# One fused attention and feed-forward kernel: two blocks of the last chunk written directly, a new written order, more adding on VectorE

## The chip, the cores and the metric

The kernel runs on one core of one Trainium2 chip. The metric is device time in microseconds (us) for one execution, the median of several runs. Beside it there is one execution recorded by the hardware profiler; its span runs from the core's first to its last instruction and is a little shorter than its time. Engines: PE (TensorE, matmuls), DVE (VectorE), ACT (ScalarE), POOL (GpSimd), SP (SyncE, which here only issues transfers).

## The reference

x has S = 2048 rows of D = 640 values in bf16. Three weight matrices make queries, keys and values for 32 heads of 20 values each; every row attends to W = 8 rows, itself and the 2nd, 4th, ... 14th row before it. Beside the attention runs a feed-forward layer of F = 1536 hidden values.

```python
x = A_x
xn = _layernorm(x)                                   # no scale, no bias
qkv = xn @ wqkv                                      # (2048, 3*640), 32 heads of 20
idx = pos[:, None] - 2 * arange(8)[None, :]          # masked where negative
logits = einsum("bhsd,bhswd->bhsw", q, kg) * 20**-0.5
o = einsum("bhsw,bhswd->bhsd", softmax(logits), vg)
ffn = gelu(xn @ w1 + b1) @ w2 + b2
return x + o @ wo + ffn
```

## The kernel before

The 2048 rows are cut into four chunks (n = 0 to 3) of 512 rows, each of four blocks of 128 rows. All weights and all of x stay on the chip. The work of a chunk is a chain of pieces, each a Python function of a few instructions with a short name; in the names the first digit is the chunk.

- st, su, sq, rs, rc, xn: layer norm of a block (statistics on DVE for chunks 0 and 1, on ACT for 2 and 3). tp and tc turn a normed block so that features lie on partitions (chunk 0: on PE, with copies; the others: a transposing transfer that SP issues, L292).
- hj and hc (chunk 0), pj and pc (the others): the projections to queries (first digit after the chunk or after hj: 0), keys (1) and values (2) on PE, and ACT's copies of them out of PSUM. ga to ge and gc are the first two blocks' queries.
- qk: DVE multiplies queries with shifted keys (L433) into two large buffers, half[0] and half[1], one for each four of the eight offsets. Five values of a head are on different 128-column tiles and must still be added: PE sums over partitions with a matmul against head_of (L479, piece lg), and either sums over the tiles as well by accumulating, or DVE adds tiles first. LEVEL[n] says how far DVE goes: at 0 PE takes five tiles, at 1 DVE adds two pairs (pa, L465) and PE takes three, at 2 one more add (pb, L470) and PE takes two, at 3 yet one more and PE takes one.
- m, mx, ex, ss, ri, at: the softmax over eight offsets (maximum, subtraction, exponential, sum, reciprocal, product). Chunk 0 does it in two parts, a and b. The exponentials and the logarithms use one table of ACT, the GELU another; changing between them is a load (L173).
- xd, xs: SP's transfers that copy each head's weights to the four partitions of the head (L563). av: DVE multiplies them with shifted values (L578). ad, ot: four DVE adds of the halves (L587, L592), whose result oT is the attention output, features on partitions.
- f1, ge: the hidden layer on PE (L599) and its GELU on ACT (L615); twelve tiles a chunk.

The outputs of chunks 0 to 2 are made turned: piece t(n)(s)(0 to 3) accumulates the hidden layer's part of 128 output columns s, t(n)(s)4 the attention's part, which needs oT (L673). u copies the result out of PSUM with b2 (ACT, L676), ut turns it back by a transposing transfer that SP issues (L680), and ud adds it onto the output in memory by an accumulating transfer that POOL issues (L685). The output rows have been filled with x before (xp).

The last chunk's outputs are made straight, block by block (bl = 0 to 3), so that nothing has to be turned at the end: o3(bl)(0 to 3) is the hidden layer's part, o3(bl)4 the attention's. A row of 640 columns takes two PSUM places, lo with 512 columns and hi with 128. For blocks 0, 1 and 2, oc copies both out on ACT (L641, L642) and od adds them to the output through POOL (L646). The last block is written directly: xl has added b2 to its x rows, oclo adds x to lo on DVE (L693) and stores 512 columns through SP (L694); ohi makes the last 128 columns on PE, ochi adds x to them (L702) and ochd stores them through ACT's queue (L707).

PSUM has eight places: psA gives four by turns to all that is tagged acc, psO two, psL one tile of two places to the logits.

The order is written out by hand: ORDER (L41 to L71) lists all pieces, and PE, DVE, ACT and SP each take the instructions of the pieces in that order, every one waiting for its inputs. A piece may hold instructions of more than one engine; oclo holds an add of DVE and a transfer of SP. In chunk 1, for instance, u13 stands in L63, u12 in L64, ut12 in L65 and ut13 in L66. POOL is not in the set of engines that keep the written order (L810); the tool that builds the program orders its instructions itself.

Of the kernel before, what the change touches and what calls it, by code (L numbers as in the profile page):

```python
# [46 lines left out]
pj113 pc113 pj103 pj111 ge0_10 pj101 pc111 pj114 ldx ge0_7 pa000 pc101 pa010 lg0 mask m0a ld2 pc103 pj102 pc114 pad11
su21 mx0a ex0a pj112 pc112 m0b mx0b ss0a pc102 ex0b ri0a ss0b pj100 pc100 at0a ri0b at0b pj110 pj104 pc104 pc110 xd0
qk111 f10_2 ge0_2 su22 qk100 hj212 hc212 f10_6 ge0_6 pj121 su20 f10_1 pc121 su23 ldo f11_10 ge1_10 ng2 ge0_1 sq20
f11_5 f10_11 pj122 pc122 f10_3 qk110 sq22 t040 qk101 f11_0 t000 lg1 xp0 av010 ge0_3 sq21 xs0 ge1_0 sq23 rs2 f10_8  # L50
ge0_8 t001 m1 f11_3 rc2 xn23 tc23 ge0_11 av031 t041 mx1 av021 xn20 tc20 f11_7 av011 ge1_5 ge1_7 av001 ge1_3 xp1 f10_9
t042 t002 xn21 ge0_9 tc21 pj120 xn22 tc22 av030 av000 f11_9 ge1_9 pj124 ex1 av020 ss1 pc120 pc124 pj123 pc123 ad00 ri1
t043 f11_2 t003 pj204 at1 pc204 xd1 su31 ad01 pad12 ad02 ot0 pj200 pc200 pj201 pc201 av101 xp2 pj212 su30 pc212 pj220
pj213 pc220 pc213 pj223 pc223 pj211 su33 pc211 pj203 su32 ng3 sq33 pad21 av100 sq31 pj202 f11_6 t004 u00 av110 xs1
av130 t044 av120 av131 av121 t010 av111 t011 t012 t013 u04 t020 t014 sq32 pc203 pc202 pj221 sq30 rs3 rc3 ad11 u01 ut00
ad10 ad12 t030 pj210 pc221 t031 t021 t022 ut01 ge1_2 pj214 xn33 tc33 t032 t033 t034 xn31 tc31 ge1_6 pj224 t023 t024
f11_8 ot1 pc214 pad22 pc210 qk201 qk211 qk210 xn30 tc30 f12_9 qk200 f11_1 pa210 pa201 xn32 ge1_8 u02 pa211 pa200 f11_4
ge1_1 t100 ge1_4 tc32 pj311 pc311 pb212 ud00 ud01 ge2_9 pj310 pc310 pad31 pj304 pc304 pj314 pc314 t101 pj300 pj324
pc324 ut02 pj303 f12_10 pb202 pc224 u03 pc303 xp3 pj301 pc301 xl ge2_10 pc300 f13_9 pj313 pc313 pj312 ud02 ut03 ud03
pj302 pc302 f13_6 ge3_6 pj323 lg2 pc312 qk300 m2 pc323 f11_11 ge1_11 f13_0 ge3_0 mx2 ut04 f13_11 ge3_9 ex2 pa300 ss2  # L60
qk310 ri2 at2 xs2 qk301 t130 t131 f12_1 ge2_1 ge3_11 t132 f13_10 qk311 t102 t103 f13_2 pa310 xd2 t104 pj320 pc320
f13_1 ge3_1 u10 ut10 ud10 f12_8 pa311 pa301 pb312 ge2_8 f13_8 ge3_8 t110 t133 t111 t112 t113 t114 u11 ge3_10 f12_5
pj222 pc222 pj321 pc321 pb302 lg3 av200 t134 u13 m3 av221 ge2_5 xb3 f12_11 t140 t141 t120 ut11 mx3 f12_2 ge3_2 av211  # L63
ex3 ss3 ri3 av220 ge2_2 f13_5 ge2_11 t142 t143 t121 t122 t123 f12_6 ge2_6 at3 xs3 f12_3 ge2_3 t124 u12 f12_7 pj322  # L64
ud04 av210 av201 av231 f12_0 t144 ge2_7 ge2_0 t200 av230 pc322 u14 ut12 ud11 f12_4 ge2_4 ge3_5 f13_4 ge3_4 o310 f13_7  # L65
ge3_7 t210 ad20 ad21 ad22 ot2 f13_3 t201 t202 pad32 av321 t203 ge3_3 o311 av331 ut13 av320 xd3 t204 u20 av300 ut14  # L66
# [8 lines left out]
def kernel(  # L75
# [544 lines left out]
    def do_o(n, bl, pc, parts):  # L620
        cs = slice(bl * P, (bl + 1) * P)
        if pc == 0 and "lo" in parts:
            for part in ("lo", "hi"):
                pool, tag = (psA, "acc") if bl % 2 else (psO, "o")
                tiles[part, n, bl] = pool.tile([P, CH], F32, tag=tag, name=part)
        lo, hi = tiles["lo", n, bl], tiles["hi", n, bl]
# [4 lines left out]
        for k, (lhs, rhs) in enumerate(srcs):
            first, last = pc == 0 and k == 0, pc == 4 and k == len(srcs) - 1
            if "lo" in parts:
                nc.tensor.matmul(lo[:], lhsT=lhs, rhs=rhs[:, 0:CH], start=first, stop=last)  # L634
            if "hi" in parts:
                nc.tensor.matmul(hi[:, 0 : D - CH], lhsT=lhs, rhs=rhs[:, CH:D], start=first, stop=last)  # L636

    def do_oc(n, bl):
        osb = outp.tile([P, D], BF16, tag="osb", name="osb")
        tiles["osb", n, bl] = osb  # L640
        nc.scalar.copy(osb[:, 0:CH], tiles["lo", n, bl][:])  # L641
        nc.scalar.copy(osb[:, CH:D], tiles["hi", n, bl][:, 0 : D - CH])  # L642

    def do_od(n, bl):
        b = n * BPC + bl
        nc.gpsimd.dma_start(out_sd[b * P : (b + 1) * P, :], tiles["osb", n, bl][:], accum_op=ALU.add)  # L646
# [41 lines left out]
    last = (NCH - 1, BPC - 1)  # L688

    def do_oclo():  # L690
        osb = outp.tile([P, D], BF16, tag="osb", name="osb")
        tiles["osb", last] = osb
        nc.vector.tensor_tensor(out=osb[:, 0:CH], in0=tiles["lo", *last][:], in1=x_sb[:, LASTB, 0:CH], op=ALU.add)  # L693
        nc.sync.dma_start(out_sd[LASTB * P :, 0:CH], osb[:, 0:CH])  # L694
# [4 lines left out]

    def do_ochi():  # L700
        osb = tiles["osb", last]
        nc.vector.tensor_tensor(  # L702
            out=osb[:, CH:D], in0=tiles["hi", *last][:, 0 : D - CH], in1=x_sb[:, LASTB, CH:D], op=ALU.add
        )

    def do_ochd():
        nc.scalar.dma_start(out_sd[LASTB * P :, CH:D], tiles["osb", last][:, CH:D])  # L707
# [41 lines left out]
    for n in range(NCH):  # L749
# [52 lines left out]
        for bl in range(BPC):  # L802
            final = n * BPC + bl == LASTB
            for pc in range(5):
                piece(f"o{n}{bl}{pc}", do_o, n, bl, pc, ("lo",) if final else ("lo", "hi"))
            if not final:
                piece(f"oc{n}{bl}", do_oc, n, bl)
                piece(f"od{n}{bl}", do_od, n, bl)
# [39 lines left out]
```

## Time and profile before

| | us |
|---|---|
| time, median of 3 runs | 210.02 (209.96 to 210.23) |
| the profiled execution's own time | 210.03 |
| its span | 208.0 |
| PE busy | 203.5 (98%) |
| DVE busy | 180.9 (87%) |
| ACT busy | 127.5 (61%) |
| POOL busy | 24.9 (12%) |
| granted PE clock | 0.999 |

The chain of work that ended last lies on PE for 66% of the span, on DVE for 21% and on ACT for 9%. In the timeline a row is a start, a duration, an engine and its line, what is written and read, how many instructions were merged into the row, and the idle time before it with what ended it. "SPq", "ACTq" are those engines' own queues of transfers: the duration there is the time to issue one, and the time to its landing is told apart.

### The profile page before, as it was taken

Reading aid. Unit: us, or ns where it says so; the run is one execution under the profiler, and the core shown is the slowest. Engines: PE = TensorE matmul, PEld = TensorE weight load, DVE = VectorE, ACT = ScalarE, POOL = GpSimd, SP = SyncE. Lnnn points to the kernel's source line nnn. Section 1 sums busy time; section 2 is a strip of 40 time slices with the busy share of each in tenths; the row PEclk is TensorE's granted clock in tenths of the full one; section 3 lists DMA queues with packets and bytes.
Section 4 is the critical chain, followed back from the end, with each engine's and each line's share of the span. In section 5 each row is a group of like instructions: output and inputs, shape, how many; then the busy total and the mean of one; then the engine's idle time right before and its main releaser. Section 6 shows DMA issues by size and latency. Waiting matters only on the chain.

```text
span 208.0 us, 2951 instructions
## 1 busy us (share of the span) xinstructions
PE 203.5 (98%) x1164; PEld 107.0 (51%) x1164; DVE 180.9 (87%) x141; ACT 127.5 (61%) x234; POOL 24.9 (12%) x37
## 2 busy tenths in 40 slices
PE   8999999999999999999999999999999999999993
PEld 3999754554445554444455544444444444445552
DVE  2598995999699999999999989999999999999201
ACT  5589968898997877877564556744658541112210
POOL 2000000000000000220020610002200402222621
PEclk9999999999999999999999999999999999999999
DMA  6994379168426075148431790086405795556753
GB/s 217 388 395 137 68 207 395 60 122 238 162 82 162 11 189 138 25 50 91 90 25 56 114 123 0 0 188 81 37 0 100 121 108 54 50 50 76 49 68 63
DMA packets 36863, 23.88 MB, mean 115 GB/s; under 512 B 24946, under 2 KB 34674, under 8 KB 36850
## 3 DMA queue, kind: packets, MB, share of 16 engines
q1 hardware_dynamic: 26320, 18.75, 34.5%
q0 software_dynamic: 8752, 2.95, 17.8%
q10 hardware_dynamic: 1778, 2.00, 2.7%
q8 instruction: 9, 0.15, 0.3%
q14 instruction: 4, 0.03, 0.0%
HBM read 10.00 MB, written 5.57 MB: 75 GB/s over the span
## 4 chain that ended last, share of the span: by engine, by line
PE 66%; DVE 21%; ACT 9%; DMA 2%; issue 1%; DVEq 0%; ACTq 0%
PE T L673 17%; PE pps L336 15%; PE hps L599 13%; PE lo L634 7%; PE gps L380 7%; DVE half L433 5%; DVE half L587 4%; DVE sums L530 3%; PE idle L446 2%; ACT L173 2%; DVE half L465 2%; DMA xnT<-xn 2%; DVE half L578 2%; ACT hT L615 2%; PE hi L636 2%; PE gps L349 1%
## 5 line engine op out<-in xcount | busy, mean ns | idle before, releaser
L599 PE MATMUL hps<-xnT,w_sb 128*128 128x512 bf16 x240 | 56.9, 379 | 0.1
L433 DVE TENSOR_TENSOR half<-qT,kT 128x5120 bf16<-128x5120 bf16 x16 | 44.3, 2820 | 1.0 <-ACT vT L400 0.7
L673 PE MATMUL T<-hT,w_sb 128*128 128x512 bf16 x180 | 43.3, 379 | 0.0
L685 POOL DMA_DIRECT2D out_dram<-x_sb x15 | 19.5, 1357 | 172.8 <-DMA x_sb<-x_sb 168.7
L599 PEld LDWEIGHTS <-w_sb 128*128 128x128 bf16 x240 | 23.3, 98 | 28.2 <-issue 1.2
L615 ACT ACTIVATE hT<-hps,bT 128x512 bf16<-128x512 f32 x36 | 24.1, 687 | 7.3 <-PE hps L599 7.2
L673 PEld LDWEIGHTS <-w_sb 128*128 128x128 bf16 x180 | 17.6, 98 | 21.1
L578 DVE TENSOR_TENSOR half<-vT,ax 128x2560 bf16<-128x2560 bf16 x16 | 23.1, 1484 | 2.4 <-PE L L479 2.4
L676 ACT ACTIVATE x_sb<-T,bT 128x512 bf16<-128x512 f32 x15 | 10.3, 687 | 23.6 <-PE T L673 23.6
L578 DVE TENSOR_TENSOR half<-vT,x_sb 128x2560 bf16<-128x2560 bf16 x16 | 22.6, 1485 | 0.0
L587 DVE TENSOR_TENSOR half<-half,half 128x5120 bf16<-128x5120 bf16 x8 | 22.3, 2820 | 0.1
L673 PE MATMUL T<-oT,wo 128*128 128x512 bf16 x75 | 18.3, 379 | 0.3 <-DVE oT L592 0.3
L336 PE MATMUL pps<-xnT,wk_sb 128*128 128x512 bf16 x75 | 18.3, 379 | 0.0
L336 PE MATMUL pps<-xnT,wv_sb 128*128 128x512 bf16 x75 | 18.3, 379 | 0.0
L336 PE MATMUL pps<-xnT,wq_sb 128*128 128x512 bf16 x75 | 18.2, 379 | 0.0
L173 ACT ACT_TABLE_LOAD x12 | 15.4, 1283 | 0.9 <-PEq L832 0.7
L465 DVE TENSOR_TENSOR half<-half 128x2048 bf16<-128x2048 bf16 x12 | 13.9, 1217 | 0.0
L336 PEld LDWEIGHTS <-wv_sb 128*128 128x128 bf16 x75 | 8.8, 117 | 7.6
L336 PEld LDWEIGHTS <-wq_sb 128*128 128x128 bf16 x75 | 8.7, 118 | 7.7 <-issue 0.4
L336 PEld LDWEIGHTS <-wk_sb 128*128 128x128 bf16 x75 | 8.8, 117 | 7.5
L263 ACT ACTIVATE xn<-x_sb,nmr,rstd 128x640 bf16<-128x640 bf16 x12 | 10.6, 916 | 3.2 <-DMA xnT<-xn 2.3
L400 ACT CAST vT<-pps 128x512 bf16<-128x512 f32 x15 | 8.5, 589 | 6.1 <-PE pps L336 6.1
(92 smaller groups left out, 241.0 us busy)
## 6 DMA issues: line engine op xcount, KB each, us to landing
w_sb<-in_B_w_dram SPq DMA_DIRECT2D x4, 960.0 KB, 10.3
ax<-attn SPq DMA_DIRECT2D x8, 256.0 KB, 4.8
x_sb<-attn SPq DMA_DIRECT2D x8, 256.0 KB, 4.6
out_dram<-x_sb POOLq DMA_DIRECT2D x15, 128.0 KB, 4.0
x_sb<-in_A_x_dram SPq DMA_DIRECT2D x1, 1280.0 KB, 6.5
out_dram<-x_sb ACTq DMA_DIRECT2D x2, 640.0 KB, 3.1
wq_sb<-in_A_wqkv_dram SPq DMA_DIRECT2D x1, 800.0 KB, 4.7
wk_sb<-in_A_wqkv_dram SPq DMA_DIRECT2D x1, 800.0 KB, 6.3
```

The source lines that it names most:

```text
L173: nc.scalar.preload_act_table_set(name)
L336: nc.tensor.matmul(ps[:], lhsT=wqkv_p[which][:, ti, to, :], rhs=xnT[:, ti, :], start=(ti == 0), stop=(ti == KT - 1),)
L380: nc.tensor.matmul(ps[:, to - a, :], lhsT=wqkv_p[which][:, ti, to, :], rhs=tiles["xnT", 0][:, ti, pair * 2 * P : (pair + 1) * 2 * P], star ...
L433: nc.vector.tensor_tensor(out=half[h][:, :, :, cs], in0=q[:, :, at].unsqueeze(1).to_broadcast([P, W // 2, KT, 2 * P]), in1=window(k, h, at ...
L465: nc.vector.tensor_tensor(out=even, in0=even, in1=odd, op=ALU.add)
L578: nc.vector.tensor_tensor(out=half[h][:, :, :, cs], in0=window(qkv_tile(n, 2), h, cs), in1=ax_view(n)[:, j, ws, :].unsqueeze(2).to_broadca ...
L587: nc.vector.tensor_tensor(out=a, in0=a, in1=b, op=ALU.add)
L599: nc.tensor.matmul(ps[:], lhsT=w1_sb[:, ti, ft * P : (ft + 1) * P], rhs=tiles["xnT", n][:, ti, :], start=(ti == 0), stop=(ti == KT - 1),)
L615: nc.scalar.activation(hT, tiles["hps", n, ft][:], ACT.Gelu_apprx_tanh, bias=bT[:, ft : ft + 1], scale=1.0)
L634: nc.tensor.matmul(lo[:], lhsT=lhs, rhs=rhs[:, 0:CH], start=first, stop=last)
L673: nc.tensor.matmul(ps[:], lhsT=lhs, rhs=rhs, start=pc == 0 and k == 0, stop=pc == 4 and k == len(srcs) - 1)
L685: nc.gpsimd.dma_start(dst, src, accum_op=ALU.add)
```

## The change

- Last chunk: DIRECT = 2, so blocks 2 and 3 are written directly. For block 2, dc adds x rows to lo and hi on DVE and dd stores all 640 columns through SP; oc32 and od32 are gone. xl now adds b2 to two blocks of x. The sums lie in a part of half[1].
- PSUM for these outputs: a psL tile of two places holds block 0's lo and the hi of blocks 0 and 1; psA gives one place each to the lo of blocks 1 and 2 and one to the hi of blocks 2 and 3; psO one to block 3's lo. Where several hi parts share a place, only the first matmul in it starts it, and the pieces are listed so that a place is read when all that was to be written in it up to then is written.
- Loads: x blocks 2 and 3 go ahead of the keys' weights and x blocks 4 to 7 ahead of the values' weights.
- LEVEL goes from (1, 0, 2, 2) to (1, 1, 2, 3): four pa pieces in chunk 1, two more pb pieces in chunk 3.
- The softmax's sum, one reduction over strided rows, becomes three adds of halves, 4 + 4, 2 + 2 and 1 + 1 offsets, in memory of the attn tile (chunk 0: in half[0]).
- ORDER is new throughout.

```diff
+DIRECT = 2
-LEVEL = (1, 0, 2, 2)
+LEVEL = (1, 1, 2, 3)
 ORDER = """
...
-tp01a gb3 tp01b tc01a tc01b gb4 gd gc0 ge tb b1 hj102 gc1 ho st02a st02 st03a hc102 gc4 st03 hj101 rs02 xn02 rs03 xn03
...
-ut20 ud12 ud13 t211 t212 t240 t213 t214 av311 u21 ud20 t241 t242 av310 av330 t220 t221 t222 t223 t224 u22 ut21 t243
-av301 ad30 ad31 o330 o331 t230 ad32 t231 t232 t233 t234 u23 ut22 ud21 t244 u24 o312 ut23 o313 ud22 ud23 ot3 o320 o321
-o322 o323 o324 oc32 od32 ut24 o314 oc31 od31 o300 o301 o302 o303 o304 o332 o333 o334 ud14 ohi ud24 oc30 od30 oclo ochi
-ochd
+tp01a gb3 tp01b tc01a tc01b gb4 gd gc0 ge tb st03a st02a st03 rs03 st02 hj101 ho rs02 xn03 xn02 b1 st13a st11a gc4
+st12a st11 st10a st12 st10 gc1 tp03 tc03 st13 tp02 tc02 hj100 hc100 hj102 hc101 hc102 pk hj112 hc112 hj110 hc110 hj212
...
+f13_5 o310 t230 ge2_5 t231 t232 pc321 ge3_5 f13_8 t201 f12_11 ge2_11 ad22 ot2 t202 pad32 av301 f13_10 ge3_10 o300 o301
+ge3_8 o302 o303 av310 t233 t203 t204 av300 u20 ud12 ut14 ud13 ud14 t234 u23 av311 ut20 ud20 t210 av331 t211 t212 av330
+av321 t213 t214 u21 t220 t221 o330 t222 ut21 t223 av320 ad30 ad31 t224 o331 o311 o332 o312 ad32 ud21 u22 t240 t241
+t242 t243 o320 t244 ot3 u24 o321 o322 o323 o313 o314 o304 oc31 oc30 o324 o333 ut22 ud22 o334 dc oclo ut23 ut24 ud23
+ohi od31 od30 dd ud24 ochi ochd
...
     load_w(0)
+    load_x(2, BPC)
     load_w(1)
-    load_x(2, BPC)
+    load_x(BPC, 2 * BPC)
     load_w(2)
-    load_x(BPC, 2 * BPC)
...
     def do_sum(n, i):
-        total = softmax_tile("sums", n, [P], F32)
-        nc.vector.tensor_reduce(
-            out=total[:, i, :], in_=tiles["e", n][:, i, :, :].rearrange("p w c -> p c w"), axis=AX.X, op=ALU.add
-        )
+        a, e = sums(n, i), tiles["e", n][:, i, :, :]
+        nc.vector.tensor_tensor(out=a, in0=e[:, 0 : W // 2, :], in1=e[:, W // 2 :, :], op=ALU.add)
+        for k in (2, 1):
+            nc.vector.tensor_tensor(out=a[:, 0:k, :], in0=a[:, 0:k, :], in1=a[:, k : 2 * k, :], op=ALU.add)
...
+    def out_ps(bl, hi):
+        first = lambda: psL.tile([P, W, P], F32, tag="L", name="tail")
+        if bl == 0 or (hi and bl == 1):
+            ps = get("tail", first)[:].rearrange("p w c -> p (w c)")
+            return ps[:, CH + bl * P : CH + (bl + 1) * P] if hi else ps[:, 0:CH]
+        key = "hi" if hi else ("lo", bl)
+        pool, tag = (psO, "o") if key == ("lo", BPC - 1) else (psA, "acc")
+        ps = get(key, lambda: pool.tile([P, CH], F32, tag=tag, name="hi" if hi else "lo"))
+        return ps[:, (bl - BPC + DIRECT) * P : (bl - BPC + DIRECT + 1) * P] if hi else ps[:]
...
+    def direct(bl, hi):
+
+        b = (NCH - 1) * BPC + bl
+        room = half[1][:].rearrange("p w t c -> p (w t c)")[:, (bl % 2) * D : (bl % 2 + 1) * D]
+        cs = slice(CH, D) if hi else slice(0, CH)
+        nc.vector.tensor_tensor(out=room[:, cs], in0=out_ps(bl, hi), in1=x_sb[:, b, cs], op=ALU.add)
+        return room, out_sd[b * P : (b + 1) * P, :]
...
+    def do_dc():
+        direct(BPC - 2, False)
+        tiles["dc"] = direct(BPC - 2, True)
+
+    def do_dd():
+        room, dst = tiles["dc"]
+        nc.sync.dma_start(dst, room)
 
     def do_oclo():
...
+        room, dst = direct(BPC - 1, False)
+        nc.sync.dma_start(dst[:, 0:CH], room[:, 0:CH])
```

More of the change, by code (lines that the diff above doesn't have):

```diff
@@ L42 @@
 pad01 pad02 st00a st00 sum1 rs00 mean1 neg1 sq1 xn00a xn00b tp00a wa tp00b wb tc00a tc00b rs01 ga xn01a xn01b gb2
-tp01a gb3 tp01b tc01a tc01b gb4 gd gc0 ge tb b1 hj102 gc1 ho st02a st02 st03a hc102 gc4 st03 hj101 rs02 xn02 rs03 xn03
-st10a st12a st13a st11a hc101 st12 hj100 hc100 hj200 tp02 tc02 tp03 tc03 pk st13 hj201 hc200 st11 st10 hj202 hc202
-hj012 hc012 hc201 rs1 rc1 hj112 hc112 xn12 tc12 xn10 hj210 qk000 hj011 hc011 tc10 hj110 hc110 qk001 hj010 hc010 hc210
-hj111 hc111 qk011 qk010 pa011 pa001 xn11 tc11 xn13 hj211 hc211 f10_5 tc13 f10_4 ge0_4 ge0_5 f10_0 ge0_0 f10_7 f10_10
@@ L47 @@
[L47 to L66, printed above, removed]
@@ new lines @@
+rs1 hj012 hj011 rc1 qk001 hc212 xn12 tc12 qk000 hc012 hj111 xn10 tc10 hc011 pa010 pa000 hj210 hc210 hc111 hj010 hc010
+hj201 qk010 qk011 pa001 pa011 xn11 tc11 xn13 tc13 hj200 pad11 f10_0 hc200 hc201 hj211 f10_5 ge0_0 f10_11 ge0_11 pj101
+pj102 pc101 pj114 pc102 pj112 hc211 pj113 ge0_5 pc114 lg0 pj111 mask m0b mx0b pj100 pc112 pc113 ldx su20 ex0b pc100
+m0a mx0a pc111 ex0a ss0b ss0a ri0b pj103 at0b pc103 ri0a at0a pj110 pc110 ld2 pj104 pc104 qk110 qk100 qk111 f10_6
+f11_0 su23 ge1_0 f10_2 f11_9 xs0 qk101 ldo xp0 ge0_6 f11_10 ge0_2 pa100 pa110 ge1_9 su22 f10_4 su21 ge0_4 pa101 pa111
@@ new lines @@
+ng2 f10_1 ge0_1 f10_7 ge0_7 sq23 f10_3 ge0_3 sq22 ge1_10 sq20 f11_3 t000 ge1_3 pj122 pj121 t001 sq21 rs2 rc2 hj202
+hc202 xd0 t040 f10_10 lg1 av010 av020 av031 av021 xn23 pc121 f10_8 tc23 m1 av030 mx1 av000 pc122 av001 f10_9 xn22 tc22
+t041 ge0_9 ge0_8 f11_1 xn20 pj124 tc20 xp1 ge1_1 ge0_10 xn21 f11_5 ge1_5 t002 ex1 ss1 pj123 pc123 av011 t003 pc124
+su33 t042 f11_7 pad21 pj120 pc120 ri1 at1 t043 pad12 tc21 pj221 pj223 pc223 xd1 pc221 pj214 pc214 pj211 ad01 xs1 xp2
+pc211 su32 pj204 pc204 pj201 pj200 pj210 ad00 su30 ad02 pc200 pc201 pc210 su31 av101 pj202 pc202 ot0 av111 av110 ng3
@@ new lines @@
+pj212 pc212 pj220 pc220 av130 sq30 pj213 f12_2 pc213 pad31 pj203 pc203 t004 u00 av120 pad22 sq31 t044 u04 t020 sq32
+sq33 rs3 f12_8 av131 t021 t010 av121 av100 t022 rc3 t023 t024 u02 ad11 ad10 ad12 ut00 ud00 xn32 tc32 xn30 tc30 t011
+t012 t013 t014 t030 ge2_2 t031 ge1_7 t032 t033 t034 xn31 tc31 f12_6 ge2_6 xn33 f12_1 ge2_1 f11_4 ge1_4 f11_2 ge1_2
+qk201 ot1 pa210 pj224 u01 f11_8 pc224 tc33 pj314 pc314 qk211 qk210 qk200 ut01 pj313 ge1_8 pa201 ut02 pa211 ge2_8 pa200
+pb212 pb202 pj311 pc311 pj300 f13_11 pc313 pj310 pc310 pj312 pc312 ge3_11 t110 f13_4 pj303 pc303 f13_9 u03 ge3_9 pj302
@@ new lines @@
+pc302 pj301 pc301 pj304 pc304 xl ge3_4 f13_6 pj320 pc300 lg2 qk300 ud01 m2 pa300 mx2 ut03 pc320 xp3 f11_11 ge1_11
+qk311 t100 f13_0 f11_6 t111 ge3_6 ge1_6 t101 ex2 t112 ss2 ud02 ud03 f12_10 f12_3 pj222 xb3 ge2_10 ri2 t102 pj324 pa311
+t103 t104 u10 t113 ge2_3 at2 xd2 ut04 t114 u11 qk310 qk301 pa301 pa310 pb302 pc222 pb312 t120 pb304 t121 t122 pb314
+t123 t124 u12 pc324 ut10 t130 t131 f13_3 ge3_0 ut11 xs2 ge3_3 f12_0 t140 f12_4 ud10 ge2_4 t141 t132 t133 lg3 av200
+ge2_0 f12_9 ge2_9 f13_7 m3 av211 ud04 mx3 ge3_7 f12_5 ex3 t134 f12_7 av220 ss3 av221 ud11 pj322 pc322 ri3 at3 ut12 xs3
@@ new lines @@
+pj323 av201 pc323 u13 ut13 ge2_7 f13_1 ge3_1 xd3 t142 t143 t144 u14 f13_2 av231 ge3_2 pj321 av210 av230 ad21 ad20 t200
+f13_5 o310 t230 ge2_5 t231 t232 pc321 ge3_5 f13_8 t201 f12_11 ge2_11 ad22 ot2 t202 pad32 av301 f13_10 ge3_10 o300 o301
+ge3_8 o302 o303 av310 t233 t203 t204 av300 u20 ud12 ut14 ud13 ud14 t234 u23 av311 ut20 ud20 t210 av331 t211 t212 av330
+av321 t213 t214 u21 t220 t221 o330 t222 ut21 t223 av320 ad30 ad31 t224 o331 o311 o332 o312 ad32 ud21 u22 t240 t241
+t242 t243 o320 t244 ot3 u24 o321 o322 o323 o313 o314 o304 oc31 oc30 o324 o333 ut22 ud22 o334 dc oclo ut23 ut24 ud23
@@ L295, in rows @@
     def rows(n):
-        cs = slice(n * BPC, min((n + 1) * BPC, LASTB))
+        cs = slice(n * BPC, min((n + 1) * BPC, LASTB + 1 - DIRECT))
         return cs, out_sd.rearrange("(b p) d -> p b d", p=P)[:, cs, :]
@@ L307, in do_xl @@
     def do_xl():
-        nc.vector.tensor_tensor(out=x_sb[:, LASTB, :], in0=x_sb[:, LASTB, :], in1=b2bc[:], op=ALU.add)
+        rows_ = x_sb[:, LASTB + 1 - DIRECT :, :]
+        nc.vector.tensor_tensor(
+            out=rows_, in0=rows_, in1=b2bc[:].unsqueeze(1).to_broadcast([P, DIRECT, D]), op=ALU.add
+        )
     def qkv_tile(n, which):
@@ L498, in softmax_tile, with attn_tile, sums @@
         return get((key, n), lambda: smp.tile([P, PARTS[n]] + [s // PARTS[n] if s == P else s for s in shape], dtype, tag=key, name=key))
+    scratch = half[0][:].rearrange("p w t c -> p (w t c)").bitcast(F32)
     def shifted(n, i):
-        cs, width = part(n, i)
         if PARTS[n] == 1:
             return tiles["L", n][:]
-        low = half[0][:].rearrange("p w t c -> p (w t c)").bitcast(F32)[:, 0 : W * P]
-        return low.rearrange("p (i w c) -> p i w c", i=PARTS[n], w=W)[:, i, :, :]
+        return scratch[:, 0 : W * P].rearrange("p (i w c) -> p i w c", i=PARTS[n], w=W)[:, i, :, :]
+    def attn_tile(n):
+        return get(("attn", n), lambda: smp.tile([P, W, P], BF16, tag="attn", name="attn"))
+    def sums(n, i):
+        if PARTS[n] == 1:
+            return attn_tile(n)[:].rearrange("p w c -> p (w c)").bitcast(F32).rearrange("p (w c) -> p w c", w=W // 2)
+        room = scratch[:, W * P : W * P + W * P // 2]
+        return room.rearrange("p (i w c) -> p i w c", i=PARTS[n], w=W // 2)[:, i, :, :]
     def do_max(n, i):
@@ L528, in do_sum @@
     def do_sum(n, i):
-        total = softmax_tile("sums", n, [P], F32)
-        nc.vector.tensor_reduce(
-            out=total[:, i, :], in_=tiles["e", n][:, i, :, :].rearrange("p w c -> p c w"), axis=AX.X, op=ALU.add
-        )
+        a, e = sums(n, i), tiles["e", n][:, i, :, :]
+        nc.vector.tensor_tensor(out=a, in0=e[:, 0 : W // 2, :], in1=e[:, W // 2 :, :], op=ALU.add)
+        for k in (2, 1):
+            nc.vector.tensor_tensor(out=a[:, 0:k, :], in0=a[:, 0:k, :], in1=a[:, k : 2 * k, :], op=ALU.add)
     def do_recip(n, i):
         rs = get(("rs", n), lambda: smp.tile([P, PARTS[n], P // PARTS[n]], F32, tag="m", name="rs"))
-        total = tiles["sums", n][:, i, :]
+        total = sums(n, i)[:, 0, :]
         table(LOG_SET)
@@ L542, in do_attn @@
         cs, width = part(n, i)
-        attn = get(("attn", n), lambda: smp.tile([P, W, P], BF16, tag="attn", name="attn"))
+        attn = attn_tile(n)
         nc.vector.tensor_tensor(
@@ L617, in do_ge, with do_o @@
         )
[L620 to L626, printed above, removed]
+    def out_ps(bl, hi):
[7 more added lines that the diff above has]
+        return ps[:, (bl - BPC + DIRECT) * P : (bl - BPC + DIRECT + 1) * P] if hi else ps[:]
+    opened = set()
+    def do_o(bl, pc, parts):
+        n, cs = NCH - 1, slice(bl * P, (bl + 1) * P)
         if pc < 4:
@@ L631, in do_o, with do_oc, do_od @@
         for k, (lhs, rhs) in enumerate(srcs):
-            first, last = pc == 0 and k == 0, pc == 4 and k == len(srcs) - 1
+            final = pc == 4 and k == len(srcs) - 1
             if "lo" in parts:
-                nc.tensor.matmul(lo[:], lhsT=lhs, rhs=rhs[:, 0:CH], start=first, stop=last)
+                nc.tensor.matmul(out_ps(bl, False), lhsT=lhs, rhs=rhs[:, 0:CH], start=pc == 0 and k == 0, stop=final)
             if "hi" in parts:
-                nc.tensor.matmul(hi[:, 0 : D - CH], lhsT=lhs, rhs=rhs[:, CH:D], start=first, stop=last)
-    def do_oc(n, bl):
-        osb = outp.tile([P, D], BF16, tag="osb", name="osb")
[L640 to L646, printed above, removed]
+                bank = bl // 2
+                first = bank not in opened
+                opened.add(bank)
+                nc.tensor.matmul(
+                    out_ps(bl, True), lhsT=lhs, rhs=rhs[:, CH:D], start=first, stop=final, skip_group_check=True
+                )
+    def do_oc(bl):
+        osb = outp.tile([P, D], BF16, tag="osb", name="osb")
+        tiles["osb", bl] = osb
+        nc.scalar.copy(osb[:, 0:CH], out_ps(bl, False))
+        nc.scalar.copy(osb[:, CH:D], out_ps(bl, True))
+    def do_od(bl):
+        b = (NCH - 1) * BPC + bl
+        nc.gpsimd.dma_start(out_sd[b * P : (b + 1) * P, :], tiles["osb", bl][:], accum_op=ALU.add)
+    def direct(bl, hi):
+        b = (NCH - 1) * BPC + bl
+        room = half[1][:].rearrange("p w t c -> p (w t c)")[:, (bl % 2) * D : (bl % 2 + 1) * D]
+        cs = slice(CH, D) if hi else slice(0, CH)
+        nc.vector.tensor_tensor(out=room[:, cs], in0=out_ps(bl, hi), in1=x_sb[:, b, cs], op=ALU.add)
+        return room, out_sd[b * P : (b + 1) * P, :]
     def spent_x(i):
@@ L685, in do_ud @@
         nc.gpsimd.dma_start(dst, src, accum_op=ALU.add)
-    last = (NCH - 1, BPC - 1)
+    def do_dc():
[4 more added lines that the diff above has]
+        nc.sync.dma_start(dst, room)
     def do_oclo():
[L691 to L694, printed above, removed]
+        room, dst = direct(BPC - 1, False)
+        nc.sync.dma_start(dst[:, 0:CH], room[:, 0:CH])
     def do_ohi():
         for pc in range(5):
-            do_o(*last, pc, ("hi",))
+            do_o(BPC - 1, pc, ("hi",))
     def do_ochi():
[L701 to L704, printed above, removed]
+        tiles["hi"] = direct(BPC - 1, True)
     def do_ochd():
-        nc.scalar.dma_start(out_sd[LASTB * P :, CH:D], tiles["osb", last][:, CH:D])
+        room, dst = tiles["hi"]
+        nc.scalar.dma_start(dst[:, CH:D], room[:, CH:D])
     pieces = {}
@@ L713, in piece @@
         pieces[name] = lambda: fn(*args)
-    for name in "tb b1 mean1 ho ldx ld2 ldo xl oclo ohi ochi ochd mask pk".split():
+    for name in "tb b1 mean1 ho ldx ld2 ldo xl dc dd oclo ohi ochi ochd mask pk".split():
         piece(name, locals()[f"do_{name}"])
@@ L802 @@
         for bl in range(BPC):
-            final = n * BPC + bl == LASTB
             for pc in range(5):
[L805 to L808, printed above, removed]
+                piece(f"o{n}{bl}{pc}", do_o, bl, pc, ("lo",) if bl == BPC - 1 else ("lo", "hi"))
+            if bl < BPC - DIRECT:
+                piece(f"oc{n}{bl}", do_oc, bl)
+                piece(f"od{n}{bl}", do_od, bl)
     engines = {getattr(mybir.EngineType, e) for e in ("PE", "DVE", "Activation", "SP")}
```

## The prediction

> **What bounds the kernel now.** I read the page's busy times and slices first, then TensorE's (PE's) row of the timeline, then the queues of the last 50 us. All sums are against one profiled execution: its span is 208.0 us and its own time 210.03 us, so 2.03 us lie around the span; the median of the runs is 210.02. 0.2% (0.4 us) is about what a measurement here can tell from no change.
>
> ```profile
> PE 203.5 (98%) x1164; PEld 107.0 (51%) x1164; DVE 180.9 (87%) x141; ACT 127.5 (61%) x234; POOL 24.9 (12%) x37
> ...
> PE   8999999999999999999999999999999999999993
> ...
> DVE  2598995999699999999999989999999999999201
> ```
>
> PE is busy in every slice but the ends, so the time is three parts: a start, PE's own matmuls, and a tail after the last matmul. The last matmul starts and ends here (PE timeline, then the other engines' last rows: DVE, ACT's queue, SP's queue, POOL):
>
> ```profile
> 204.37 0.44 PE L636 MATMUL hi<-wo,oT 128*128 128x128 bf16 x5
> ...
> 204.84 0.29 DVE L702 TENSOR_TENSOR osb<-hi,x_sb 128x128 bf16<-128x128 f32 x1 [0.20 <-PE hi L636]
> ...
> 205.17 0.36 ACTq L707 DMA_DIRECT2D out_dram<-osb  x1
> ...
> 160.11 2.52 SPq L680 DMA_TRANSPOSE x_sb<-x_sb  x2
> 162.67 1.23 SPq L563 DMA_DIRECT2D x_sb<-attn  x2
> 164.42 27.08 SPq L680 DMA_TRANSPOSE x_sb<-x_sb  x6
> 204.67 0.35 SPq L694 DMA_DIRECT2D out_dram<-osb  x1
> ...
> 193.02 2.59 POOL L685 DMA_DIRECT2D out_dram<-x_sb  x2 [3.73 <-DMA x_sb<-x_sb]
> ```
>
> PE ends at 204.81; the tail is 208.0 - 204.8 = 3.2 us: one small add, one small store, its landing. See also what is not in it: the last transposes (L680) were issued by 191.5, 13 us before SP's store of the last block's first columns.
>
> SP takes its list strictly in turn, and the rows show what that costs. ACT wrote u12 and u13 here:
>
> ```profile
> 147.49 0.69 ACT L676 ACTIVATE x_sb<-T,bT 128x512 bf16<-128x512 f32 x1 [1.82 <-PE T L673]
> ...
> 159.39 0.69 ACT L676 ACTIVATE x_sb<-T,bT 128x512 bf16<-128x512 f32 x1 [0.39 <-PE T L673]
> ...
> SPq L694 <- DVE osb L693: 13.1, 1, 13.1
> ```
>
> The list (L63 to L66) has u13 before u12, so the first row is u13's, but ut12 ahead of ut13; the transposes went out together, ut12 at 160.11 (u12 ended at 160.08) and ut13 behind it. ut13 stood 13 us with its data ready. The last line (waits of SP's queue) is the store of oclo: SP stood 13.1 us before it, with nothing behind it.
>
> **The change, part by part.**
>
> *Logits (LEVEL).* Chunk 1's logits go from 40 matmuls to 24, chunk 3's from 16 to 8. The rows of L479 give 2.27 us for 40 (53.67 to 55.94), 1.41 for 24, 0.98 for 16, so 0.86 + 0.49 = 1.35 us less for PE, all on its path: -1.35.
>
> *What DVE pays before ot3.* Four pa1 adds at 1.155 (4.62 for four, L465) and two pb3 at 1.14 (L470): +6.9. xl doubles, 0.48 to about 0.8 (by 2560 elements in 1.49): +0.3. The five sums (three of 1.92, two of 1.06) become three adds each: 0.69 for 512 outputs (L544, L516), 0.29 for 128 (L702), 0.42 between: about 1.2 and 0.75 with overlap, -2.2; bounds -3 (if the first add ran as L465 does, two per cycle) and 0. Net +5.0, hidden as long as ot3 is in time. It ended at 193.76. b1 moves behind six other DVE pieces, so DVE's 1.95 us wait for tb goes; then ot3 ends near 196.8. PE needs it at o314, with o314, o304, o324 (1.35 each), o333 (0.65), o334 (1.08) and ohi (0.93) still to do, 6.7 us before the end, at 196.8. Level; the waits of DVE at lg1, lg2 and lg3 (1.69, 0.71, 0.75), some of which the new order shortens, are the margin. Cost taken 0, bounds 0 and +2 (no wait regained).
>
> *lg1.* PE has one f1 and one t piece more ahead of lg1 (1.73 us), so it comes there at 55.4; DVE, which finished chunk 1's products at 53.3, finishes them with pa1 at 53.3 - 1.95 - 0.2 + 4.6 = 55.7. PE waits 0.3 (bounds 0 and 0.6).
>
> *Loads.* x blocks 2 and 3 (320 KB) now stand ahead of the keys' weights, x 4 to 7 (640 KB) ahead of the values'. In the old order x 2 and 3 landed 6.6 us after 2.23, at 8.8, last of this group; the same bytes end then, so the keys' weights land at 8.8 instead of 8.0; PE wants them at 9.53. The values' weights land at 12.5 (as x 4 to 7 did); the first piece that needs them, hj212, comes after hj101, tp03, tp02, hj100, hj102, hj112, hj110 (4.9 us of matmuls), at 14.4. Both covered: 0. If the first cover failed, PE would lose that lateness, some tenths; bounds 0 and +0.5.
>
> *ACT.* The list changes activation tables 14 times instead of 12 (+2.6 us), and oc32's copies go (-0.86). ACT is busy 61%; 0.
>
> *PSUM.* Block 1 of the last chunk holds one rotating place instead of two while f1 pieces still run; f1's rows show 0.1 us idle in all, so at most -0.1. Two blocks' last 128 columns share a place; dc has read block 2's 1.7 us before PE's end, and ohi, which writes block 3's, starts 0.93 before it: 0.
>
> *Block 2 written directly.* dc (0.69 + 0.29) falls where DVE stood 10.2 us idle; dd's store of 160 KB is one of the steps below.
>
> *The tail.* Here the order of the list decides. The new list has ut22, oclo, ut23, ut24, dd on SP. oclo's store waits for DVE's add, which waits for o334, PE's last but ohi; ut23 and ut24, whose data ACT has written 9 us before PE's end (t244 is followed by 9.95 us of matmuls), are queued behind it, and POOL's ud23 and ud24 wait for them. Counted from PE's new end, E:
> - oclo's store as now at E - 0.14 (204.67), SP busy 0.35: E + 0.21.
> - ut23 at E + 0.25, ut24 1.3 later (160.11 and 161.4) at E + 1.57; landing 2.3 (that pair) to 2.6 and 3.5 (the last pair): ut23 E + 2.6 to 3.8, ut24 E + 3.9 to 4.2.
> - POOL starts some 0.5 behind a landing (162.4, 162.98): ud23 E + 3.1 to 4.3; ud24 not before E + 4.4, and 0.8 to 1.3 after ud23: E + 4.4 to 5.5; taken 4.7.
> - ud24 lands 3.7 to 4.6 after its start (L685; the pairs 3.8 and 4.1, 3.9 and 4.6); taken 4.1: E + 8.8.
> - The span ends 1.35 after the last landing (ACT's store 205.17 + 1.5 = 206.65, end 208.0): E + 10.15, bounds E + 9.4 and E + 11.4.
> dd's store goes at E + 2.9 and lands by E + 5, inside this.
>
> The Trainium skill's DMA: Bandwidth & Descriptors, Latency and other measured facts, gives a DMA about 2 us of fixed cost. By it ud24 would land 2 instead of 4.1 us after its start, an estimate of 2.1 us less, 213.6; L685's rows, never under 3.7, speak against it and are used.
>
> *Sum.* E = 204.81 - 1.35 + 0.3 = 203.75, less 0.2 for PE's two small waits of now at oT and lg3 (0.28, 0.17) of which half should go: 203.6. Span 203.6 + 10.15 = 213.75, time + 2.03 = 215.8 us, against 210.03: +5.7, of which tail +6.95, PE -1.2.
>
> **Rivals.**
> *A, not slower: the transposes are not held.* If a later transpose passes a waiting store on SP's queue, the tail stays 3.2: 203.6 + 3.2 + 2.03 = 208.8 (-0.6%). For it: the data are there 9 us early, and in the trace nothing ever stood behind such a store. Against it: ut13's 13 us behind ut12. It decides from ut24 issued at E - 3.7 or sooner (2.4 to land, 0.5, 4.1, 1.35 make 8.3, against 3.2 + 1.35 allowed). Chance 0.09.
> The Trainium skill's Perfetto Trace Analysis, DMA Instruction - HWDGE (DVE, Sync), says that DMA engines could wait on semaphores but on trn2 do not: the sequencer waits. The trace agrees (13.1 us at SP's store).
>
> *B, POOL's order.* POOL isn't in the written order; before, ud24 stood ahead of od32, od31 and od30 though listed later. If ud23 and ud24 stand so again, od31 and od30 go behind them, 1.28 + 0.87 after ud24's start, landing 3.6 later: E + 4.7 + 2.15 + 3.6 + 1.35 = E + 11.8, 217.4. Against: od31's and od30's copies come 5 us before oclo. Chance 0.15.
>
> *C, DVE becomes the bound.* None of its waits is regained and ot3 comes 2 us late: 217.8. For: DVE 87% busy and 5 us more; against: the wait for tb, whose place in the list is filled. Chance 0.12.
>
> **How the numbers follow.** The forecast has 0.64, A 0.09, B 0.15, C 0.12. The time is the forecast's, 215.8. Its own bounds are E + 9.4 (215.0) and E + 11.4 (217.0); with PE's own bounds (0.5 sooner, if it waits nowhere; 0.8 later, with the bounds of lg1 and the loads), POOL's start as close behind a landing as at 193.02 (0.1 instead of 0.5 after 190.3 + 2.6), and B and C, the range is 214.0 to 218.2. A stays out. Faster 0.08, same 0.02 (A with a partly longer tail), slower 0.90.
>
> **What would show it.** Right: ut23 and ut24 start behind SP's last-block store, after PE's last matmul; POOL's last rows some 4 to 5 us after it; PE's last slices empty; L479 with x72; PE's end 203 to 204; span minus PE's end near 10. Wrong: SP's last row a store of 128 KB or of 160 KB with all transposes before PE's end (A); POOL's last rows from osb (B); a PE wait for oT at o314 (C); or PE ending later than before, from waits for weights near 10 us or for PSUM places, which I priced at nothing.

## The result, and the profile after

The changed kernel takes 215.20 us (median of 4 runs, 215.09 to 216.57) against 209.99: a ratio of 1.026 with a 95% interval of 1.022 to 1.030, 5.2 us slower. Forecast were 215.8 (214.0 to 218.2) and slower. The profiled execution took 215.09 with a span of 212.7.

The page's busy times and slices of the changed kernel:

```profile
PE 201.9 (95%) x1140; PEld 106.4 (50%) x1140; DVE 186.7 (88%) x159; ACT 129.1 (61%) x234; POOL 24.0 (11%) x36
...
PE   8999999999999999999999999999999999999910
...
POOL 2000000000000000200040220042200221320322
```

PE did less than before (201.9 instead of 203.5 us) and fills every slice but the last two, where POOL now works instead. The timeline's last rows on PE, DVE, SP's queue, ACT's queue and POOL, after the change:

```profile
202.27 0.44 PE L661 MATMUL hi<-wo,oT 128*128 128x128 bf16 x5
...
192.79 0.69 ACT L711 ACTIVATE x_sb<-T,bT 128x512 bf16<-128x512 f32 x1 [6.72 <-PE T L708]
...
201.80 0.69 DVE L680 TENSOR_TENSOR half<-lo,x_sb 128x512 bf16<-128x512 f32 x1 [0.89 <-PE lo L656]
...
202.52 0.35 SPq L733 DMA_DIRECT2D out_dram<-half  x1
202.96 2.56 SPq L715 DMA_TRANSPOSE x_sb<-x_sb  x2
205.58 0.57 SPq L729 DMA_DIRECT2D out_dram<-half  x1
...
203.07 0.36 ACTq L744 DMA_DIRECT2D out_dram<-half  x1
...
205.81 1.30 POOL L720 DMA_DIRECT2D out_dram<-x_sb  x1 [4.77 <-DMA x_sb<-x_sb]
207.34 1.30 POOL L720 DMA_DIRECT2D out_dram<-x_sb  x1 [0.23 <-issue]
```

PE ends at 202.71 (204.81 before). u24, the last input of a transpose, was written by 193.48. Yet the two transposes start at 202.96, right behind SP's store of oclo at 202.52, which waited for DVE's add at 201.80. ud23 and ud24 follow on POOL, and the span ends at 212.7. The tail after PE is 10.0 us instead of 3.2. The waits of SP's queue give the same:

```profile
SPq L733 <- DVE half L680: 15.1, 1, 15.1
```

SP stood 15.1 us before that store, as it stood 13.1 us before. The difference is what was queued behind it.

### The profile page after: what moved, and what is told of

Read it like the earlier page. It is cut to its first block, busy times and chain, and to the rows that moved or that the text cites. A ratio compares the mean times of both kernels' runs of the same rounds, so it can differ in the third digit from the quotient of the medians.

```text
span 212.7 us, 2934 instructions
## 1 busy us (share of the span) xinstructions
PE 201.9 (95%) x1140; PEld 106.4 (50%) x1140; DVE 186.7 (88%) x159; ACT 129.1 (61%) x234; POOL 24.0 (11%) x36
## 4 chain that ended last, share of the span: by engine, by line
PE 95%; DMA 1%; issue 1%; POOLq 1%; POOL 0%; DVE 0%; SPq 0%
PE T L708 26%; PE hps L613 25%; PE pps L340 23%; PE gps L384 6%; PE lo L656 5%; PE idle L450 2%; PE L L483 2%; PE tail L656 2%; PE gps L353 1%; DMA x_sb<-x_sb 1%; PE tail L661 1%; PE tp L281 1%; POOLq L879 1%; PE hi L661 0%; POOL out_dram L720 0%
## 5 line engine op out<-in xcount | busy, mean ns | idle before, releaser
L708 PE MATMUL T<-hT,w_sb 128*128 128x512 bf16 x180 | 43.9, 379 | 0.0
L720 POOL DMA_DIRECT2D out_dram<-x_sb x15 | 19.5, 1381 | 170.3 <-DMA x_sb<-x_sb 170.0
L469 DVE TENSOR_TENSOR half<-half 128x2048 bf16<-128x2048 bf16 x16 | 18.8, 1219 | 0.0
L340 PE MATMUL pps<-xnT,wk_sb 128*128 128x512 bf16 x75 | 17.8, 379 | 0.0
L340 PE MATMUL pps<-xnT,wq_sb 128*128 128x512 bf16 x75 | 17.7, 379 | 0.0
L404 ACT CAST kT<-pps 128x512 bf16<-128x512 f32 x15 | 8.7, 588 | 5.7 <-PE pps L340 5.6
L404 ACT CAST qT<-pps 128x512 bf16<-128x512 f32 x15 | 8.7, 584 | 5.7 <-PE pps L340 5.7
```

The source lines that it names most:

```text
L340: nc.tensor.matmul(ps[:], lhsT=wqkv_p[which][:, ti, to, :], rhs=xnT[:, ti, :], start=(ti == 0), stop=(ti == KT - 1),)
L404: nc.scalar.copy(dest[:, to, off : off + CH], tiles["pps", n, which, to][:])
L469: nc.vector.tensor_tensor(out=even, in0=even, in1=odd, op=ALU.add)
L708: nc.tensor.matmul(ps[:], lhsT=lhs, rhs=rhs, start=pc == 0 and k == 0, stop=pc == 4 and k == len(srcs) - 1)
L720: nc.gpsimd.dma_start(dst, src, accum_op=ALU.add)
```

## The experiments

Some of these runs began with the queries' weights landing up to 2 us late, which moves all of PE's work by as much; it shows as a wait for wq_sb in PE's first rows. Where that matters, the runs are compared by PE's end less that shift, or by their lowest times.

**The transposes first (e1).** Only two names move in the list.

```diff
-ut22 ud22 o334 dc oclo ut23 ut24 ud23
+ut22 ut23 ut24 ud22 o334 dc oclo ud23
```

> Only the places of ut23 and ut24 in the new list change: they stand right behind ut22, ahead of oclo. Theory (SP's list order is the whole slowdown): SP issues both before 197, since u24 is written at 193.5; POOL's ud24 lands by 202; PE ends at 202.7 as in the changed kernel, the tail is 3.2 again, the span 205.9, the time about 208.2, so 1.8 us faster than the kernel before. Rival 1 (the tail comes from two blocks written directly, or from POOL's adding transfers being last in any order): the tail stays near 10 and the time near 215. Rival 2 (transposes and stores disturb each other, order or not): between the two, 210 to 213.

Measured: 208.70 us, ratio to the kernel before 0.994 (0.992 to 0.996). Run again beside three others (e11):

> The same kernel as e1, as the measure for the three beside it on the same chip: 208.7 within 0.3, where the first weights land at 5.8 to 5.9; later by as much as they land later.

It gave 208.92 (lowest 208.38), ratio 0.995 (0.991 to 0.999). SP's queue in e1, timeline:

```profile
176.91 17.72 SPq L715 DMA_TRANSPOSE x_sb<-x_sb  x5
202.46 0.35 SPq L733 DMA_DIRECT2D out_dram<-half  x1
202.86 0.42 SPq L729 DMA_DIRECT2D out_dram<-half  x1
```

All transposes are out by 194.63, PE ends at 202.65 (202.71 in the changed kernel), and the tail is 3.75 (span 206.4). The move of two names is worth 6.5 us of 215.2. The tail stayed 0.5 above the expected one: ACT's last store took 2.2 us to land instead of 1.5. With this the rest of the change is a gain, and this kernel is the fastest of all, 0.6% below the one before.

**The kernel before with the transposes last (e2).** The same fault put into the old list.

```diff
-t244 u24 o312 ut23 o313 ud22 ud23 ot3
+t244 u24 o312 o313 ud22 ot3
...
-oc32 od32 ut24 o314
+oc32 od32 o314
...
-ohi ud24 oc30 od30 oclo ochi
+ohi oc30 od30 oclo ut23 ut24 ud23 ud24 ochi
```

> The kernel before, with ut23 and ut24 moved behind oclo in its list (ud23 and ud24 with them), nothing else. Theory: PE still ends at 204.8, and the tail grows from 3.2 to about 10, by the same steps as in the changed kernel: time 216.5 to 217.5, 6.5 to 7.5 us slower. Rival (the price of 7 us belongs to the changed kernel's way of ending): the kernel before stays within 1 us of 210.

Measured: 216.97 us (median of three of four executions, 216.78 to 217.31), ratio 1.033 (1.031 to 1.035), 7.0 us. The price needs nothing else of the change. The only profile of e2 is of the remaining execution, whose PE was slow throughout (last section). It has the steps in the same order: SP's store at 1212.66, the two transposes from 1213.12, POOL's adding transfers at 1215.97 and 1217.52, the end at 1223.1.

**The store by another queue (e3).** The list as changed, only oclo's store is ACT's.

```diff
-        nc.sync.dma_start(dst[:, 0:CH], room[:, 0:CH])
+        nc.scalar.dma_start(dst[:, 0:CH], room[:, 0:CH])
```

> The changed kernel with its list as it is, but oclo's store of 512 columns goes through ACT's queue instead of SP's. Theory (what holds the transposes is the store that waits at the head of SP's queue): nothing stands in front of ut23 and ut24, they go out by 197, the time is 208.2 to 208.7 (ACT issues two stores at the end, 0.36 us each). Rival (the place in the list holds them, whatever queue the store uses): 215, as the changed kernel.

Measured: 209.03 us (0.994 to 0.997 of the kernel before), 0.3 above the expected range. SP's and ACT's queues, timeline:

```profile
176.80 17.71 SPq L715 DMA_TRANSPOSE x_sb<-x_sb  x5
200.76 0.35 SPq L729 DMA_DIRECT2D out_dram<-half  x1
...
202.35 0.36 ACTq L733 DMA_DIRECT2D out_dram<-half  x1
202.90 0.36 ACTq L744 DMA_DIRECT2D out_dram<-half  x1
```

With the waiting store gone from SP, the transposes leave early though they stand behind oclo in the list. So it is the wait at the head of SP's queue. A place in the list behind oclo holds the transposes only while oclo's store is SP's, too.

**One transpose held (e4).** ut23 moved ahead, ut24 left behind oclo.

```diff
-ut22 ud22 o334 dc oclo ut23 ut24 ud23
+ut22 ut23 ud22 o334 dc oclo ut24 ud23
```

> The changed kernel with ut23 moved behind ut22 and ut24 left behind oclo: half the dose. Theory: ut24 is issued 0.25 after PE's end instead of 1.6, and POOL has one adding transfer after it instead of two. ut24 lands at PE's end + 2.6, ud24 starts at + 3.1 and lands at + 7.0, the span ends at + 8.5: time 213.5, 1.6 less than the changed kernel. So 6.5 of the 7 us are the chain of one transpose and one adding transfer, not their number. Rival (each held transpose costs its share): half way, 211.7.

Measured: 213.79 us, ratio 1.018 (1.016 to 1.020). SP's queue and POOL, timeline:

```profile
202.94 1.20 SPq L715 DMA_TRANSPOSE x_sb<-x_sb  x1
...
205.96 1.32 POOL L720 DMA_DIRECT2D out_dram<-x_sb  x1 [5.01 <-DMA x_sb<-x_sb]
```

The steps after PE's end (202.62) are those forecast within 0.3: transpose + 0.3, adding transfer + 3.3, end of the span + 8.6. One held transpose costs 5.1 us against e1, the second only 1.4 more: most of the price is the chain, not the count. (The expectation's "6.5 of the 7 us" is a slip: its own steps, + 8.5 against a tail of 3.2, make 5.3.)

**The logits as before (e5).** On e1, the six added DVE pieces left out and PE's 24 matmuls back.

```diff
-LEVEL = (1, 1, 2, 3)
+LEVEL = (1, 0, 2, 2)
```

> On top of the list with the transposes first (e1, 208.7): LEVEL back to (1, 0, 2, 2), so the four pa1 and the two new pb3 pieces are left out and PE takes 24 logits matmuls more; the rest of the list as it is. Theory: the logits' rows are PE's own path and give 0.85 (chunk 1) and 0.43 (chunk 3) back: PE ends near 203.9 instead of 202.65, time 210.0. Rival: DVE, freed of 6.9 us, ends its waits elsewhere and the gain of the matmuls was not the path: 208.7.

Measured: 210.89 us (lowest 210.34), ratio 1.004 (1.000 to 1.007). PE's first rows show a late start:

```profile
8.06 1.03 PE L352 MATMUL gps<-xnT,wq_sb 128*128 128x128 bf16 x15 [1.69 <-DMA wq_sb<-in_A_wqkv_dram]
```

In e1 this row starts at 6.10. Of the 3.08 us by which PE ends later (205.73 against 202.65), 1.89 are there when lg1 starts. Behind lg1 it is 2.75 us behind e1, and lg3 takes it from 2.65 to 3.09. So the logits cost 0.86 and 0.44 us, as their rows say. PE gets the matmuls' time back in full, and in e1 it waits for none of the six adds.

**The sum by one reduction (e6).** On e1, do_sum as before the change.

```diff
-        a, e = sums(n, i), tiles["e", n][:, i, :, :]
-        nc.vector.tensor_tensor(out=a, in0=e[:, 0 : W // 2, :], in1=e[:, W // 2 :, :], op=ALU.add)
-        for k in (2, 1):
-            nc.vector.tensor_tensor(out=a[:, 0:k, :], in0=a[:, 0:k, :], in1=a[:, k : 2 * k, :], op=ALU.add)
+        total = softmax_tile("sums", n, [P], F32)
+        nc.vector.tensor_reduce(
+            out=total[:, i, :], in_=tiles["e", n][:, i, :, :].rearrange("p w c -> p c w"), axis=AX.X, op=ALU.add
+        )
```

> On top of e1: the softmax's sum is one strided reduction again, 2.2 us more DVE work before ot3 in all (three of 1.92 for three of 1.27, two of 1.06 for two of 0.8). In the changed kernel oT is ready at 195.58 and o314's attention matmuls start at 195.80. Theory (the prediction's step that DVE is level with PE at ot3): nothing is left to hide it, PE waits at o314 for oT, 1.5 to 2 us, time 210.2 to 210.7. Rival: DVE's own waits at the logits shrink by as much and the time stays 208.7.

Measured: 209.31 us, 0.6 above e1, where 1.5 to 2 were expected; ratio 0.996 (0.993 to 0.999). The last piece of the attention on DVE (ot3) in e1, then a wait of PE and ot3 in e6:

```profile
194.01 1.49 DVE L606 TENSOR_TENSOR oT<-half 128x2560 bf16<-128x2560 bf16 x1
```

```profile
72.32 1.24 PE L340 MATMUL pps<-xnT,wk_sb 128*128 128x512 bf16 x5 [0.38 <-ACT vT L404]
...
194.79 1.49 DVE L606 TENSOR_TENSOR oT<-half 128x2560 bf16<-128x2560 bf16 x1
```

oT came 0.78 later, not 2.2. Most of the miss is the size. From the start of a sum to the start of DVE's next piece, the reduction takes 0.47, 0.44 and 0.44 us more than the three adds in chunks 1, 2 and 3, and 0.05 more in all of chunk 0: 1.4 us. The 2.2 had let the three adds overlap. They do not: the first ends at 69.12 in the changed kernel, the second starts at 69.15. The rest is waits that shrank: DVE's idle time before chunk 2's first product with the values went from 1.00 to 0.55 and the one at lg1 from 0.69 to 0.64, and DVE began 0.1 sooner in e6. PE's 0.62 (end 203.27 instead of 202.65) is 0.38 at 72.32, where ACT's copies came late, and some 0.25 at o314.

**The loads as before (e7, e12).** On e1, the five loads in the old order.

```diff
     load_w(0)
-    load_x(2, BPC)
     load_w(1)
-    load_x(BPC, 2 * BPC)
+    load_x(2, BPC)
     load_w(2)
+    load_x(BPC, 2 * BPC)
```

> On top of e1: the loads in the old order (keys' weights, x 2 and 3, values' weights, x 4 to 7), the list unchanged. x 2 and 3 land at 8.8 instead of 6.7 and DVE's statistics of block 3, which now start at 7.63 (blocks 2 and 3 take 2 us and the normed rows of block 3 follow 0.3 later), start 1.2 later; tp03 on PE starts at 10.68 now and would start near 11.6. Theory: PE loses about 0.9 us there and carries it to the end, time 209.6. Rival (the prediction priced the loads at nothing; the list has room early): 208.7.

> e7 again beside e1 on the same chip. e7 ran with the first weights landing 1.1 late, which moved x 2 and 3 as well; PE waited 1.02 us for ACT's statistics of block 3 all the same. Theory: with undisturbed loads x 2 and 3 land at 8.8, PE waits about 0.9 at tp03, and the time is e1's plus 0.9 to 1.1. Rival: e1's within 0.3, the wait being an effect of the late weights.

Measured: e7 210.96 us (ratio 1.004, 1.000 to 1.007), e12 210.92 (lowest 209.78; 1.001, 0.998 to 1.004). PE's two long waits near the start in e12:

```profile
7.11 1.03 PE L353 MATMUL gps<-xnT,wq_sb 128*128 128x128 bf16 x15 [1.28 <-DMA wq_sb<-in_A_wqkv_dram]
...
12.68 0.99 PE L281 MATMUL tp<-ident,xn 128*128 128x128 bf16 x10 [0.97 <-ACT rstd L249]
```

In e11 the first of these rows starts at 6.09 and no wait follows. PE's end is 204.99 in e12 and 202.56 in e11, 2.43 later, of which 1.02 are the first row's: 1.4 us are the loads, where 0.9 to 1.1 were expected. tp03 starts another 1.1 later, its ten matmuls take 0.99 instead of 0.72 us, and behind them PE is the whole 2.43 behind. The lowest times say the same (209.78 and 208.38). Late weights alone don't make this wait: e5 and e10 have the new loads, began as late (8.06 and 7.27), and PE waits for nothing at tp03. The new list needs the new loads: it asks for blocks 2 and 3 before the second half of the keys.

**Block 2 by ACT and POOL again (e8, e9).** On e1; xl and the rows that xp and xb fill are again those of DIRECT = 1.

```diff
-... o334 dc oclo ud23 ohi od31 od30 dd ud24
+... o334 oc32 od32 oclo ud23 ohi od31 od30 ud24
...
-            if bl < BPC - DIRECT:
+            if bl < BPC - 1:
```

> On top of e1: block 2 of the last chunk by ACT's copies and POOL's adding transfer again (oc32, od32, its x rows through xp3 and xb3), PSUM places and list otherwise as in the change. od32's copies end 1.9 before PE's end, POOL starts it 0.3 later, it lands 3.6 to 4 after that, 2.0 to 2.4 after PE's end; the last store lands 2.5 after PE's end in e1. Theory: writing block 2 directly is worth nothing in the tail, 208.7 within 0.3. Rival: the adding transfer lands last and later, behind od31 and od30 on POOL, 209.5 or more.

Measured: 211.57 us (lowest 210.35), ratio 1.006 (1.003 to 1.009). ACT and PE near the end, timeline:

```profile
204.07 0.59 ACT L665 CAST osb<-lo 128x512 bf16<-128x512 f32 x1 [3.15 <-DMA out_dram<-osb]
204.55 0.27 ACT L666 CAST osb<-hi 128x128 bf16<-128x128 f32 x1
...
204.88 0.49 PE L658 MATMUL hi<-w_sb,wq_sb 128*128 128x128 bf16 x6 [1.83 <-ACT osb L666]
```

This does not price the direct writing: the third copy had to wait for the first of two buffers, and PE waited for the copy, though ohi writes other columns of that place. With a third buffer:

```diff
-    outp = ctx.enter_context(tc.tile_pool(name="outp", bufs=2))
+    outp = ctx.enter_context(tc.tile_pool(name="outp", bufs=3))
```

> e8 with three instead of two buffers for ACT's copies. In e8 ACT's copy of block 2 waited 3.15 us for the landing of od31's transfer, which held the first of two buffers, and PE waited 1.8 us at ohi for that copy, since blocks 2 and 3 share a PSUM place. Theory: with a third buffer ACT copies block 2 by 1.9 before PE's end, PE waits nowhere, and od32 lands about 2.4 after PE's end, like the last store: the time is that of e1 within 0.3. Rival: POOL's third adding transfer lands last, 1 us or more after the store: 209.7 or more.

Measured: 209.17 us (lowest 208.90), ratio 0.995 (0.992 to 0.998), against 208.92 (208.38) for e11 beside it. The medians differ by 0.25 us, the lowest times by 0.52, and the intervals overlap: writing block 2 directly is worth half a microsecond at most, which these runs don't tell from nothing. It spares a third buffer.

**Block 2's store first (e10).** dd right behind dc in e1's list.

```diff
-ut22 ut23 ut24 ud22 o334 dc oclo ud23 ohi od31 od30 dd ud24
+ut22 ut23 ut24 ud22 o334 dc dd oclo ud23 ohi od31 od30 ud24
```

> e1 with dd, the store of block 2, ahead of oclo in the list, so that it leaves SP at 200.9 instead of 202.86. In e1 ACT's last store took 2.15 us to land (1.5 in the kernel before), with two other stores under way. Theory (the three last stores share the transfer engines): dd is nearly done by 202.5, the last store lands in 1.7, the time is 208.3. Rival (what slows them is od31 and od30, under way until 204): no change against e1, as the early dd of e3 landed at 204.97 all the same.

Measured: 209.18 us (lowest 208.48), ratio 0.997 (0.993 to 1.001): no gain over e11. The store left 1.6 us ahead of oclo's instead of 0.4 behind it, but it took 3.9 us to land (2.0 in e11), until 207.4, and ACT's last store landed at 207.8, 2.6 us after PE's end (2.4 in e11). So the early store was under way almost to the end all the same, and e10 doesn't decide between its two theories. What slows the last stores stays open.

## Why the prediction was right

*The tail.* Forecast from PE's end: oclo's store - 0.14, transposes + 0.25 and + 1.57, adding transfers + 3.1 to 4.3 and + 4.7, end + 10.15. Measured: - 0.19, + 0.25 and + 1.6, + 3.1 and + 4.63, + 10.0. The adding transfers landed 3.8 us after their starts (4.1 was taken), the end came 1.55 behind the last landing (1.35). (One of the fifteen such transfers before took 7.5 us, which the bounds left out.) e1, e2, e3 and e4 show the mechanism: SP takes its instructions in turn, and a store that waits for PE's last outputs holds what stands behind it. The estimate from the Trainium skill's 2 us of fixed cost for a DMA (DMA: Bandwidth & Descriptors, Latency and other measured facts) comes to 213.7, not 213.6; the 3.8 us of L720 decide against using it alone here.

*PE.* Forecast -1.2, measured -2.1: this step was mis-sized. The rows before with PE's old waits, then lg1 and lg3 after:

```profile
81.86 2.32 PE L673 MATMUL T<-oT,wo 128*128 128x512 bf16 x10 [0.28 <-DVE oT L592]
...
145.22 1.05 PE L479 MATMUL L<-half,head_of 128*32 128x512 bf16 x16 [0.17 <-DVE half L470]
...
155.71 2.57 PE L599 MATMUL hps<-xnT,w_sb 128*128 128x512 bf16 x10
```

```profile
55.42 1.48 PE L483 MATMUL L<-half,head_of 128*32 128x512 bf16 x24
...
147.69 0.61 PE L483 MATMUL L<-half,head_of 128*32 128x512 bf16 x8
```

The logits gave what the rows said (2.27 to 1.42 us for chunk 1, 0.98 to 0.55 for chunk 3, -1.28). But I took 0.3 for a wait at lg1 that measures 0.1: I let PE wait for DVE's last add (it ends at 55.59), while lg1 reads half[0] first and starts at 55.42. And I let only half of PE's old waits go. All went: 0.28 at oT, 0.17 at lg3, and 0.25 in the ten f1 matmuls at 155.71 (2.57 us, where other rows of ten take 2.32), which I had not counted. That makes 1.9; the other 0.2 is not traced.

*The time around the span.* The sum carried 2.03 us over from the kernel before. In the changed kernel it is 2.39, and 2.4 to 2.5 in the other executions; no run shows why. This 0.4 goes against PE's 0.9 and the tail's 0.15, so the sum misses by 0.7 (215.8 against 215.09) where its terms miss by 1.4 in all: in part luck.

*DVE.* "Level" at ot3 was right: oT is there at 195.58 and PE takes it at 195.80 (196.8 forecast for both). It was right for a partly wrong reason, as e6 says: the sums save 1.4 us and not 2.2, and DVE regained 1.0 us of its wait at lg1 (1.69 to 0.68) besides tb's. At lg3 its wait grew (0.75 to 0.99). The 0.71 that the prediction puts at lg2 ended with a copy of ACT and is still there (0.54).

*Loads, ACT, PSUM, block 2.* Priced at nothing, and PE shows no wait for them: the keys' weights landed at 8.8 (8.8 forecast), the values' at 12.5 (12.5). e7 and e12 add what the prediction didn't say: the new loads carry the new list, 1.4 us would be lost without them.

*Rivals.* A (transposes not held) fell: the changed kernel and e2 show them held, and e3 shows what lets them go. (Its limit for ut24, E - 3.7, counts the 1.35 behind the last landing twice; with the tail of 3.2 it is E - 5.1. No run comes near either.) B (POOL's order) fell: od31 and od30 stood ahead of ud23 and ud24, at 199.27. C (DVE the bound) fell in the changed kernel by 0.2 us of margin.

The two parts of the change pulled apart: with the transposes freed (e1) the rest of it makes the kernel 1.2 us faster than before (208.70 against 209.94). By e5 the logits are worth 1.3 us of that, so the other parts together come to about nothing.

## What to carry to other kernels

Read a written order engine by engine, and for each queue that waits ask what stands behind the waiting instruction and whose data is long ready; a store of the very last result belongs at the end of its queue, or on a queue with nothing behind it. The price of such a place is the whole chain behind the held instruction (here a transpose, an adding transfer and their landings, 5 to 7 us), not its own issue time. When PE is busy without a gap, as here, matmuls taken from it come back one for one (e5) as long as the engine that takes the work over has margin at the next hand-over; work that margin out at that point.
